# Moving part of an output product, half a matmul slot and a PSUM bank in a segment-recurrent attention kernel

## Chip, core and metric

The kernel runs on one core of a Trainium2 chip. The metric is device time in microseconds of one execution; the median of three runs of the kernel before is 957.34.

## What is computed

The reference has two blocks. Block A is attention over segments with a recurrent memory, block B a feed-forward network. Both have a residual connection around them and a layer norm (without gain) ahead of them. Cut to what matters here:

```python
# A: x (1,2048,640), 32 heads of 128, memory of M=8 rows, segments of 32 tokens -> 64 steps
mem = mem0
for s in range(64):
    h = concat([mem, x[:, 32*s:32*s+32]])            # 40 rows
    q, k, v = h@Wq, h@Wk, h@Wv                       # 32 heads x 128
    scores = q @ k.T * scale; masked: row i sees memory, and tokens up to itself
    o = softmax(scores) @ v @ Wo                     # 40 x 640
    mem = o[:, :8]                                   # goes into the next step
    outs.append(o[:, 8:])
# B: relu(x@w1 + b1)**2 @ w2 + b2
```

The next step's memory rows come out of this step's output product, so the 64 steps run one after the other.

## The kernel before

Only the memory rows and the first 24 tokens of a segment (`HD = 24`) are projected inside the step. The last 8 tokens of four segments (`TL = 8`) are projected together ahead of time as "tail units". Such units, and the output product of tail rows, stand in a list `fill`; `run(fill, n)` puts n of them into the instruction stream at fixed places of a step. A projection unit is one 128-row chunk of the contraction: four matmuls of 512 columns.

**Matmul shape.** Nearly all products of a step have 32 rows of output. They use a quarter of TensorE's columns: `proj` issues for each chunk c the four matmuls k = 0 to 3, each into 32 partitions of one PSUM tile, `ps[32*k:32*k+32, :]`. The scores do so for four groups g. In the profile these are the rows with `128*32`.

**One step** (`step(b, sp)`, s = 4b + sp) on PE, in the order in which the program issues it; all engines run their own queues in program order:

1. q0, k0, q1, k1: four projections (L234), 20 matmuls each. q1 goes into `potile(1)`, k0 into the one bank `ch`, the others into the pool `mm` of three banks.
2. scores(0) of the memory rows (L495), bank `ch`; the product v, first half, into `potile(0)`, 8 matmuls; token_scores(0) (L587); v first half, 12 more. ACT copies it out (L594).
3. v second half into an `mm` tile, first chunk: 4 matmuls; scores(1), bank `ch`, 16; second chunk, 4; token_scores(1), 16; last three chunks, 12. ACT copies it out (L608).
4. Some fill units; values(0) for the memory rows (L537 and L542; it needs pB0 from soft3); more fill units; values(1) (needs pB1 from soft2(1), L521).
5. The output product pw (`wo_rounds`, L270): 16 rounds of four plus four matmuls of 320 columns, in bank `ch`. Rounds 0 to 7 read the first half of the heads in `oT`, 8 to 15 the second half. ACT casts the first half of oT from values(0) (L246), DVE the second from values(1) (L244).
6. The rest of the fill units, then token_values of the step before (L421, L426).

On DVE and ACT the softmax of the memory rows runs beside this: soft1 is mx (DVE L501) and em (ACT L504), soft2 is rm, em, pm (DVE L510 to L518) and for n = 1 the transpose into pB1 (L521), soft3 is pT and four copies into pB0 (L526 to L529). After values(1), DVE has in its queue: causal mask (L612, issued before its cast of oT), cast of oT (L244), mxk, tk (L642, L644), zk, rk (L651, L653), and then `wo_out`: ACT copies two blocks of pw to otmp (L285, L286), DVE adds them (o, L287) and `mem_to_hT` transposes o into hT (L380), in two parts. The next step's q0 waits for hT.

All of this is an order written out by hand (`manual_schedule`). Step 0 (`ready`) and step 63 (`last`) differ; 62 steps in between have the form above.

Of the kernel before, what the change touches and what calls it, by code (L numbers as in the profile page):

```python
# [11 lines left out]
F32 = mybir.dt.float32  # L12
# [4 lines left out]
def kernel(  # L17
# [19 lines left out]
    M = A_mem0.shape[1]  # L37
# [12 lines left out]
    NK = SEG + M  # L50
# [13 lines left out]
    chn = ctx.enter_context(tc.tile_pool(name="chn", bufs=1, space=bass.MemoryType.PSUM))  # L64
# [11 lines left out]
    wv = wts.tile([128, DC * HE], BF16)  # L76
# [25 lines left out]
    oT = const.tile([128, H, NK], BF16)  # L102
# [5 lines left out]
    def head(p):  # L108

        n, g, j = p // 16, p // 4 % 4, p % 4  # L110
        return g * HG + j * 2 + n
# [59 lines left out]
    def rows_of(b, sp):  # L171
        at = HD + sp * SEG
        return lambda c: hTs[b % 2][:, c * CW + at:c * CW + at + SEG]
# [47 lines left out]
            nc.scalar.copy(out=rows_in(b).rearrange("p c (s t) -> p c s t", s=4)[:, :, :, 0:HD], in_=ptv[:, :, :, 0:HD])  # L221
        return out

    def proj(w, by, lhs, n, ps, c0, c1):

        if by == "columns":
            wr = w[:].rearrange("p (c g j n k e) -> p c n k g j e", c=DC, g=G, n=2, j=4, k=4)
        elif by == "half":
            wr = w[:].rearrange("p (c k j n e) -> p c n k j e", c=DC, k=G, n=2, j=4)
        else:  # L230
            wr = w[:].rearrange("p (c k n f) -> p c n k f", c=DC, k=G, n=2)
        for c in range(c0, c1):
            for k in range(4):
                nc.tensor.matmul(ps[32 * k:32 * k + 32, :], lhsT=lhs(c), rhs=wr[:, c, n, k], start=(c == 0), stop=(c == DC - 1))  # L234

    def mmtile():
        return mm.tile([128, 512], F32, tag="mm", name="ps")

    def potile(h):
        return pop.tile([128, 2, 512], F32, tag="po%d" % h, name="px%d" % h)[:, 0, :]  # L240
# [21 lines left out]
    def wo_rounds(lhs, pw, hs):  # L262

        for h in hs:
            for kh in range(2):
                for ch in range(2):
                    j = kh * 2 + ch
                    p = h // 8 * 16 + kh * 8 + h % 8
                    c0 = 32 * (1 - kh)
                    nc.tensor.matmul(pw[32 * j:32 * j + 32, c0:c0 + DH], lhsT=lhs(p), rhs=wov2[:, head(p), ch],  # L270
                                     start=(h == 0), stop=(h == 15))
# [22 lines left out]
    def run(q, n, held=None, stop=False):  # L294
        while n > 0 and q:
            out = q.pop(0)()
            if out and held is not None:
                held.append(out)
                if stop:
                    break  # L300
            elif out:
                out[1]()
            n -= 1
# [10 lines left out]
    def settle(held, tails):  # L314
        for out in [o for o in held if o[0] == tails]:
            held.remove(out)
            out[1]()
# [96 lines left out]
    def token_values(s, v, vt4, po):  # L414

        sp = s % 4
        pTk, pTx = back.pop()
        for i in range(HG):
            for g in range(G):
                r = slice(32 * g, 32 * g + 32)  # L420
                nc.tensor.matmul(po[0][g][:, i * 32:(i + 1) * 32], lhsT=v[r, i * E:(i + 1) * E], rhs=pTk[r, i, :],  # L421
                                 start=(i == 0), stop=False, skip_group_check=True)
        for u in range(2):
            for g in range(G):
                r = slice(32 * g, 32 * g + 32)
                nc.tensor.matmul(po[0][g][:, u * 128:(u + 1) * 128].rearrange("p (j q) -> p j q", q=32)[:, :, 0:TL],  # L426
                                 lhsT=vt4[r, sp, u, :], rhs=pTx[r, u], start=False, stop=True, skip_group_check=True)

    def token_out(s, po):
        for h in range(2):  # L430
            gs = slice(2 * h, 2 * h + 2)
            nc.scalar.copy(out=oTg[:, gs, :, :, 0:SEG],  # L432
                           in_=po[1][h][:, :, 0:256].rearrange("p g (n j q) -> p g n j q", n=2, q=32))
        nc.gpsimd.tensor_copy(out=oTts[s // 4 % 2][:, :, s % 4 * TL:(s % 4 + 1) * TL], in_=oT[:, :, 0:TL])
# [17 lines left out]
    def step(b, sp, v=None):  # L452
        s = b * 4 + sp
        last = s == NS - 1
        lhs = rows_of(b, sp)
        ready = v is not None
# [67 lines left out]
        def soft3(pm):  # L524
            pT = s1.tile([128, 2, 32], BF16, tag="pTt", name="pT")[:].rearrange("p u k -> p (u k)")
            nc.vector.transpose(out=pT, in_=pm)  # L526
            for g, copy in enumerate((nc.vector.tensor_copy, nc.scalar.copy, nc.gpsimd.tensor_copy, nc.gpsimd.tensor_copy)):
                r = slice(32 * g, 32 * g + 32)
                copy(out=pBs[0][r, g], in_=pT[r])  # L529
            return pBs[0]  # L530

        def values(n, pB, po):
            cols = po[:, 0, 0:128]
            for j in range(4):
                i = n * 4 + j
                for k in range(4):
                    nc.tensor.matmul(cols[32 * k:32 * k + 32].rearrange("p (g i m) -> p i g m", g=G, i=4)[:, j],  # L537
                                     lhsT=v[:, i * E + 32 * k:i * E + 32 * k + 32],
                                     rhs=pB[:, :, SEG + j * M:SEG + (j + 1) * M],
                                     start=(j == 0), stop=False, skip_group_check=True)  # L540
            for k in range(4):
                nc.tensor.matmul(cols[32 * k:32 * k + 32].rearrange("p (g a) -> p g a", g=G), lhsT=vt4[:, sp, n, 32 * k:32 * k + 32], rhs=pB[:, :, 0:SEG],  # L542
                                 start=False, stop=True, skip_group_check=True)
# [39 lines left out]
        def token_scores(n):  # L583
            skv = view()
            for j in range(4):
                for g in range(G):
                    nc.tensor.matmul(skv[32 * g:32 * g + 32, n * 4 + j, :], lhsT=qT[:, n * 16 + g * 4 + j, :],  # L587
                                     rhs=kT[:, n * 16 + g * 4 + j, :], start=True, stop=True,
                                     skip_group_check=True)

        token_scores(0)
        if not ready:
            proj(wv, "half", lhs, 0, ps0, 2, DC)
            nc.scalar.copy(out=v[:, 0:512], in_=ps0[:])  # L594
            ps1 = mmtile()
            proj(wv, "half", lhs, 1, ps1, 0, 1)
        if not last:
            pm0 = soft2(0)
            scores(1)
            soft1(1)  # L600
            pT0 = soft3(pm0)
        if not ready:
            proj(wv, "half", lhs, 1, ps1, 1, 2)
        token_scores(1)
        if not ready:
# [5 lines left out]
        def causal(skv):  # L611
            nc.vector.tensor_tensor(out=skv[:, :, M:NK], in0=skv[:, :, M:NK],  # L612
                                    in1=mask[:].unsqueeze(1).to_broadcast([128, HG, SEG]), op=ALU.add)
# [7 lines left out]
        if last:  # L621
            run(fill, max(1, (len(fill) - 3) // 2), held, True)
            token_values(s - 1, *prevs[-2], po)
            token_out(s - 1, po)
            settle(held, True)
            run(fill, 2, held)
            settle(held, True)
            causal(skv)
        else:
            ahead = 0 if ready else (len(fill) + 1) // 2  # L630
            left = len(fill) - ahead
            run(fill, ahead // 2, held, True)
            values(0, pT0, po[1][0])
            values_out(0, po[1][0])
            run(fill, len(fill) - left, held)
            values(1, pT1, po[1][1])
            causal(skv)
            values_out(1, po[1][1])
            settle(held, True)
# [19 lines left out]
                                op=ALU.mult)  # L659

        if not last:
            pw = chn.tile([128, 512], F32, tag="ch", name="pw")
            if ready:
                for k in range(4):
                    run(fill, SEG0[k])
                    wo_rounds(lambda p: oT[:, p, M:NK], pw, [2 * k + h for h in (0, 1, 8, 9)])
            else:
                wo_rounds(lambda p: oT[:, p, M:NK], pw, range(16))
            o = wo_out(pw, ((s + 1) // 4, (s + 1) % 4))
            if s > 1:  # L670
                store_main(o, s - 2)
            held = []
            run(fill, 100, held)
            if s:
                token_values(s - 1, *prevs[-2], po)
                token_out(s - 1, po)
            settle(held, True)
            for _, f in held:
                late.append((0.35, f, s + 1))
            tails_in((s + 1) // 4, (s + 1) % 4)  # L680
# [284 lines left out]
    for t in range(S // NT):  # L965
# [8 lines left out]
        for fc in range(FC):  # L974
            ps = mmtile()
# [8 lines left out]
            w = NT if fc < FFULL else HT  # L984
# [3 lines left out]
            if more and fc >= 1 and (fc - 1) // 3 < NK4:  # L988
                k, stage = divmod(fc - 1, 3)
# [30 lines left out]
        for q in range(NK4):  # L1020
# [6 lines left out]
            for hh in range(2):  # L1027
                k = pr + 2 * hh
# [44 lines left out]
```

## Time and profile before

| | us |
|---|---|
| median of 3 runs | 957.34 (956.87 to 958.79) |
| the profiled execution | 956.46 |
| its span in the profile | 954.60 |
| PE busy | 923.6 |
| DVE busy | 703.6 |
| ACT busy | 552.3 |
| POOL busy | 309.5 |

The span is the time from the first to the last instruction of the profiled execution; 1.86 us lie around it. "Busy" is the time in which at least one instruction of an engine runs. Matmuls overlap and their ends are modelled, so a busy PE can still be waiting for something; where that matters, the starts of matmuls in the timeline are compared with the time that the ones before them take. The granted TensorE clock was 0.998 of full speed over the run. The recurrent steps take most of the span, some 12 us each; the feed-forward network comes at the end.

### The profile page before, as it was taken

The numbers are of one execution on the slowest core, as the hardware profiler recorded it, in microseconds if no ns is written. First come the engines' busy times: TensorE is split into PE (matmuls) and PEld (weight loads), VectorE is DVE, ScalarE is ACT, GpSimd is POOL, SyncE is SP. The second block draws the span as 40 slices with busy tenths as digits, with TensorE's granted clock in tenths as the row PEclk, the third lists the DMA queues.
The fourth block names the chain that finished last, engine by engine and source line by source line (L and its number), as shares of the span: only waits on it lengthen the run. The fifth ranks groups of instructions, "written<-read, shape, count | busy, mean of one in ns | idle before, by whom it ended". The sixth has DMA issues, their size and how long they took to land.

```text
span 954.6 us, 55984 instructions
## 1 busy us (share of the span) xinstructions
PE 923.6 (97%) x24760; PEld 544.0 (57%) x24760; DVE 703.6 (74%) x2131; ACT 552.3 (58%) x1460; POOL 309.5 (32%) x1002
## 2 busy tenths in 40 slices
PE   5979999999999999999999999999999999999998
PEld 2445555655565656556565656565655555555555
DVE  5168888778877887877877787878787788556632
ACT  2546666666666666666666666666666666523321
POOL 2123333333333333333333333333333333353300
PEclk9999999999999999999999999999999999999999
DMA  9983201010101000100101010101010221633320
GB/s 352 402 265 70 38 18 27 16 30 13 23 20 28 16 21 24 21 25 11 34 17 23 14 31 14 32 12 33 8 32 8 54 43 21 203 108 88 94 56 28
DMA packets 65875, 56.66 MB, mean 59 GB/s; under 512 B 37384, under 2 KB 61712, under 8 KB 63712
## 3 DMA queue, kind: packets, MB, share of 16 engines
q1 hardware_dynamic: 65392, 52.74, 19.6%
q8 instruction: 194, 3.18, 1.4%
q14 instruction: 49, 0.40, 0.1%
q0 software_dynamic: 224, 0.33, 0.1%
q10 hardware_dynamic: 16, 0.01, 0.0%
HBM read 38.37 MB, written 9.44 MB: 50 GB/s over the span
## 4 chain that ended last, share of the span: by engine, by line
PE 80%; ACT 6%; DVE 5%; DMA 5%; SPq 2%; issue 1%; ACTq 0%
PE ps L234 23%; PE pw L270 15%; PE px L234 14%; PE pk L234 7%; PE y L1030 6%; PE ps L978 6%; ACT v L594 3%; PE ps L270 2%; DMA wq<-in_A_Wq_dram 2%; PE po L421 2%; ACT em L504 2%; SPq L151 2%; DVE pm L518 2%; PE po L537 2%; DVE pB L521 2%
## 5 line engine op out<-in xcount | busy, mean ns | idle before, releaser
L234 PEld LDWEIGHTS <-hT 128*32 128x32 bf16 x7680 | 178.9, 96 | 161.2 <-DVE hT L380 24.3
L270 PE MATMUL pw<-wo,oT 128*32 128x320 bf16 x4224 | 157.7, 299 | 2.5 <-DMA wo<-in_A_Wo_dram 1.0
L270 PEld LDWEIGHTS <-oT 128*32 128x32 bf16 x4224 | 120.0, 96 | 22.8 <-issue 3.7
L258 DVE STREAM_TRANSPOSE qT<-row 128x512 bf16<-128x512 bf16 x128 | 89.5, 699 | 44.1 <-ACT row L253 43.7
L234 PE MATMUL ps<-wv,hT 128*32 128x512 bf16 x1260 | 91.9, 377 | 0.0
L649 ACT ACTIVATE ek<-tk 128x320 bf16<-128x320 f32 x64 | 30.1, 470 | 101.9 <-DVE tk L644 101.9
L655 POOL TENSOR_TENSOR pkt<-ek,rk 128x64 bf16<-128x64 bf16 x64 | 18.8, 294 | 212.1 <-ACT otmp L286 176.0
L234 PE MATMUL px<-wv,hT 128*32 128x512 bf16 x1260 | 85.2, 377 | 0.0
L234 PE MATMUL ps<-wq,hT 128*32 128x512 bf16 x1260 | 81.3, 383 | 3.3 <-DVE hT L380 2.8
L234 PE MATMUL ps<-wk,hT 128*32 128x512 bf16 x1280 | 80.0, 379 | 0.0
L234 PE MATMUL px<-wq,hT 128*32 128x512 bf16 x1260 | 78.9, 379 | 0.0
L234 PEld LDWEIGHTS <-hTt 128*32 128x32 bf16 x1920 | 54.4, 97 | 42.2 <-issue 10.1
L234 PE MATMUL pk<-wk,hT 128*32 128x512 bf16 x1240 | 77.7, 379 | 0.0
L986 ACT ACTIVATE wv<-ps,b1f 128x512 bf16<-128x512 f32 (+1 forms) x56 | 37.6, 672 | 67.0 <-PE ps L978 66.5
L432 ACT CAST oT<-po 128x512 bf16<-128x512 f32 x128 | 68.7, 589 | 8.2 <-PE po L426 2.5
L441 POOL COPY qz<-qT 128x96 bf16<-128x96 bf16 x126 | 33.4, 265 | 111.4 <-DVE qT L258 111.4
L285 ACT COPY otmp<-pw 64x96 f32<-64x96 f32 (+2 forms) x129 | 28.8, 223 | 54.0 <-PE pw L270 33.4
L1030 PE MATMUL y<-wq,wk 128*128 128x320 bf16 x416 | 58.9, 299 | 0.2
L482 ACT CAST row<-ps 128x256 bf16<-128x256 f32 x126 | 40.7, 375 | 30.0 <-PE ps L234 29.1
L253 ACT ACTIVATE row<-ps 128x512 bf16<-128x512 f32 x93 | 54.8, 613 | 5.3 <-PE ps L234 4.0
L253 ACT ACTIVATE row<-px 128x512 bf16<-128x512 f32 x63 | 37.6, 597 | 32.2 <-PE px L234 32.2
L537 PEld LDWEIGHTS <-v 128*32 128x32 bf16 x2016 | 34.1, 94 | 34.7 <-issue 15.6
(138 smaller groups left out, 1886.1 us busy)
## 6 DMA issues: line engine op xcount, KB each, us to landing
wv<-in_A_Wv_dram SPq DMA_DIRECT2D x5, 1024.0 KB
wq<-in_A_Wq_dram SPq DMA_DIRECT2D x5, 1024.0 KB
wk<-in_A_Wk_dram SPq DMA_DIRECT2D x5, 1024.0 KB
wo<-in_A_Wo_dram SPq DMA_DIRECT2D x8, 640.0 KB
o_all<-o SPq DMA_DIRECT2D x256, 7.5 KB
vt<-vt_d SPq DMA_DIRECT2D x60, 64.0 KB
xt<-in_A_x_dram SPq DMA_DIRECT2D x19, 160.0 KB
wq<-in_B_w_dram SPq DMA_DIRECT2D x1, 2080.0 KB
```

Source lines behind the costliest of these rows:

```text
L234: nc.tensor.matmul(ps[32 * k:32 * k + 32, :], lhsT=lhs(c), rhs=wr[:, c, n, k], start=(c == 0), stop=(c == DC - 1))
L253: nc.scalar.mul(out=row, in_=ps, mul=scale)
L258: nc.vector.transpose(out=dst[:, n * 16:(n + 1) * 16, 0:32], in_=row.rearrange("p (h e) -> p h e", e=32))
L270: nc.tensor.matmul(pw[32 * j:32 * j + 32, c0:c0 + DH], lhsT=lhs(p), rhs=wov2[:, head(p), ch], start=(h == 0), stop=(h == 15))
L432: nc.scalar.copy(out=oTg[:, gs, :, :, 0:SEG], in_=po[1][h][:, :, 0:256].rearrange("p g (n j q) -> p g n j q", n=2, q=32))
L441: nc.gpsimd.tensor_copy(out=d.rearrange("p a (j f) -> p a j f", j=3)[:, :, :, 0:M], in_=src[:, :, 0:3, :])
L482: nc.scalar.copy(out=row[:, u * 256:(u + 1) * 256], in_=ps[:, u * 256:(u + 1) * 256])
L537: nc.tensor.matmul(cols[32 * k:32 * k + 32].rearrange("p (g i m) -> p i g m", g=G, i=4)[:, j], lhsT=v[:, i * E + 32 * k:i * E + 32 * k + 3 ...
L649: nc.scalar.activation(out=ek[:], in_=tk[:], func=ACT.Exp, scale=1.0)
L978: nc.tensor.matmul(ps[:], lhsT=w1[:, c, fc * 128:(fc + 1) * 128], rhs=hnT[:, c, :], start=(c == 0), stop=(c == DC - 1))
L986: nc.scalar.activation(out=r[:, 0:w], in_=ps[:, 0:w], func=ACT.Relu, bias=b1f[:, fc:fc + 1], scale=1.0)
L1030: nc.tensor.matmul(y[hh][:, 0:DH], lhsT=f1T[:, fc, k * 128:(k + 1) * 128], rhs=w2[:, fc, cs], start=(fc == 0 and not hf), stop=(fc == FFUL ...
```

## The change

Three edits, in the 62 steps of the ordinary form:

- The second half of v goes into `potile(1)`, the bank that q1 used earlier in the step, and takes no tile of the pool `mm`.
- Of the first chunk of that product, only matmuls k = 0 and 1 stand ahead of scores(1); k = 2 and 3 follow the scores, ahead of the second chunk. `proj` gets an argument `ks` for that.
- The tile pw is taken earlier, and rounds 0 and 1 of the output product (8 of 64 matmuls) are issued between the second group of fill units and values(1). The other 14 rounds stay where they were.

No instruction is added or taken away.

```diff
-    def proj(w, by, lhs, n, ps, c0, c1):
+    def proj(w, by, lhs, n, ps, c0, c1, ks=range(4)):
...
         for c in range(c0, c1):
-            for k in range(4):
+            for k in ks:
                 nc.tensor.matmul(ps[32 * k:32 * k + 32, :], lhsT=lhs(c), rhs=wr[:, c, n, k], start=(c == 0), stop=(c == DC - 1))
...
-            ps1 = mmtile()
-            proj(wv, "half", lhs, 1, ps1, 0, 1)
+            ps1 = potile(1)
+            proj(wv, "half", lhs, 1, ps1, 0, 1, range(2))
         if not last:
             pm0 = soft2(0)
             scores(1)
             soft1(1)
             pT0 = soft3(pm0)
         if not ready:
+            proj(wv, "half", lhs, 1, ps1, 0, 1, range(2, 4))
             proj(wv, "half", lhs, 1, ps1, 1, 2)
...
             run(fill, len(fill) - left, held)
+            pw = chn.tile([128, 512], F32, tag="ch", name="pw")
+            if not ready:
+                wo_rounds(lambda p: oT[:, p, M:NK], pw, range(2))
             values(1, pT1, po[1][1])
...
         if not last:
-            pw = chn.tile([128, 512], F32, tag="ch", name="pw")
...
-                wo_rounds(lambda p: oT[:, p, M:NK], pw, range(16))
+                wo_rounds(lambda p: oT[:, p, M:NK], pw, range(2, 16))
```

## The prediction

> **What bounds the kernel now.** I read the page first. PE is busy 97% of the span and holds 80% of the chain that ended last; the other engines have room.
>
> ```profile
> PE 923.6 (97%) x24760; PEld 544.0 (57%) x24760; DVE 703.6 (74%) x2131; ACT 552.3 (58%) x1460; POOL 309.5 (32%) x1002
> ...
> PE 80%; ACT 6%; DVE 5%; DMA 5%; SPq 2%; issue 1%; ACTq 0%
> ...
> L270 PE MATMUL pw<-wo,oT 128*32 128x320 bf16 x4224 | 157.7, 299 | 2.5 <-DMA wo<-in_A_Wo_dram 1.0
> L1030 PE MATMUL y<-wq,wk 128*128 128x320 bf16 x416 | 58.9, 299 | 0.2
> ```
>
> The last two lines decide this case. A matmul of 320 columns that fills a quarter of the array (128*32) lasts 299 ns, exactly as long as one that fills all of it (128*128). The first kind still costs only 157.7/4224 = 37 ns, the second 58.9/416 = 142 ns. So four quarter matmuls run side by side in one slot, and a quarter matmul by itself is no shorter than the slot. For 512 columns the timeline below gives the slot: 12 matmuls, three slots, from 418.99 to 419.63, so 0.215 us.
>
> PE's busy share hides its stops, since the ends are modelled. The waits name them:
>
> ```profile
> PEld L234 <- DVE hT L380: 24.3, 67, 1.5
> ...
> PE po L537 <- DVE pB L521: 3.4, 15, 0.5
> ...
> PE ps L234 <- ACT v L608: 2.4, 11, 0.2
> ```
>
> PE waits for the next step's rows (hT), for the second softmax of the memory rows (pB), and for the copy of v, which holds a buffer that a fill tile wants. The true sizes come from starts in the timeline. An ordinary step, first:
>
> ```profile
> 418.35 0.39 PE L234 MATMUL ps<-wv,hT 128*32 128x512 bf16 x4
> 418.57 0.27 PE L495 MATMUL sm<-kT,qz 128*32 128x40 bf16 x16
> 418.67 0.39 PE L234 MATMUL ps<-wv,hT 128*32 128x512 bf16 x4
> 418.88 0.27 PE L587 MATMUL ps<-kT,qT 128*32 128x40 bf16 x16
> 418.99 0.82 PE L234 MATMUL ps<-wv,hT 128*32 128x512 bf16 x12
> 419.63 0.60 PE L234 MATMUL ps<-wv,hTt 128*32 128x512 bf16 x8
> 420.06 0.27 PE L537 MATMUL po<-pB,v 128*32 128x32 bf16 x16
> 420.17 0.23 PE L542 MATMUL po<-pB,vt 128*32 128x128 bf16 x4
> 420.22 0.60 PE L234 MATMUL ps<-wv,hTt 128*32 128x512 bf16 x8
> 421.00 0.28 PE L537 MATMUL po<-pB,v 128*32 128x32 bf16 x16 [0.17 <-DVE pB L521]
> ...
> 421.15 2.36 PE L270 MATMUL pw<-wo,oT 128*32 128x320 bf16 x64
> 423.32 1.00 PE L270 MATMUL ps<-wo,oTt 128*32 128x320 bf16 x24
> ```
>
> The two fill slots from 420.22 are done at 420.65, yet the second memory values start at 421.00: 0.35 us idle, of which the view owns to 0.17. The same reading over the 62 steps that change gives 12.7 us in all before the second values. A step with the buffer wait:
>
> ```profile
> 407.98 0.28 PE L537 MATMUL po<-pB,v 128*32 128x32 bf16 x16
> 408.09 0.24 PE L542 MATMUL po<-pB,vt 128*32 128x128 bf16 x4
> 408.55 0.62 PE L234 MATMUL ps<-wk,hTt 128*32 128x512 bf16 x8 [0.23 <-ACT v L608]
> ```
>
> L542 issues its 128 columns in 0.05, so the fill could have gone at 408.14 and lost 0.41. Such waits sum to 6.5 us, in 18 steps, and are over 0.3 in 15 of them. Waits before the first values sum to 2.7.
>
> **Split of a slot (second scores "two matmuls sooner").** No matmul is added. But the slot at 418.35 now holds two of its four matmuls, and the scores follow. The scores' first matmul needs the quarter that the slot's first one occupies for 0.215, and matmuls start in program order in every row I looked at; so it starts at 418.57, as before, and two quarters stand idle. The other two matmuls then start at 418.67 with the first two of the next chunk; that chunk's last two take one slot more, from 418.88. All later PE work of the step is 0.215 us behind: 62 × 0.215 = 13.3 us, before what the waits swallow. By the Trainium skill (TensorE: Matmul & The Clock Gate, Part 3, "The mechanism") "MATMULs are pc-monotone in start AND end — strict FIFO, no reordering"; by that rule the price is the same 0.215, and the trace's order of starts agrees. Bounds for the price: nothing, if the scores can pass; two slots, 0.43, if the halves of the two chunks don't pair. I take one slot, by the two rows of the page. Even sooner scores would help little: em(1) on ACT starts at 419.22, and the copy of v's first half, ahead of it in ACT's queue, ends at 419.16 (418.57 plus 0.585).
>
> **Odd value product in the second query bank.** It leaves the three-buffer pool, so the fill tile no longer waits for the copy of v. Its new bank was read last by the copy of the odd q, over at 404.47 in the step where the product begins at 406.01: 1.5 us of cover, and its price, were that gone, would be the lateness itself. The second values share the bank, but need that copy of v anyway.
>
> **Two rounds ahead.** Eight of the 64 pw matmuls, 2 × 0.135 = 0.27 us (64 in 421.15 to 423.32), move before the second values. They use only the first half of oT, written by ACT's cast (L246), so PE has a new wait there; behind it are queued the second values, the rest of pw, and through them DVE's cast of oT, mxk, tk, zk, rk and then o, which makes hT. Their bank was last read by em(1), over at 419.60 in the step above and so 1.4 us before. No DMA and no POOL instruction moves.
>
> **An ordinary step, retimed.** The fill starts at 419.85, the first values at 420.28, the second fill ends at 420.86. The last v matmuls end at 419.81 + 0.215 = 420.02, and v's copy (ACT, 419.90 to 420.48 now) starts at 420.08. The cast of oT (420.45 to 420.72) follows the first values: 420.67 to 420.94. With 0.06 of hand-over (pB ends 420.95, values 421.00) the rounds start at 421.00, after 0.14 of waiting, and end at 421.27. The second values start at 421.27 instead of 421.00. pw has 56 left, 14 slots, 1.89 us, from 421.42: ended at 423.31, against 423.32. PE is level; the early rounds have paid for the slot. DVE is not: its cast of oT and all behind it shift by 0.27. rk ended at 423.92, and o started at 424.06, behind ACT's otmp. DVE starts an unrelated operation some 0.08 before the last one's end (causal 420.86, pB end 420.95), so there is 0.22 of slack: o and hT come 0.05 later, and hT released the next step at 424.69. Cost +0.05.
>
> **The step with the buffer wait.** Values(0) had waited from 407.72 to 407.98, which takes the slot in. The fill runs at 408.14 to 408.57. ACT's casts don't move (v 407.91, oT 408.39 to 408.66). Rounds 408.72 to 408.99; values(1) at 409.01, as now. pw ends 0.27 sooner, rk doesn't, and o moves from 412.08 to rk's end less 0.07, 411.86: −0.22.
>
> **Sum.** Of the 62 steps, 16 are like the first (wait before the second values over 0.3): 16 × 0.05 = 0.8. In 31 that wait is smaller and less is there to be swallowed; the same retiming gives +0.115 in the mean, 3.6. The 15 with the buffer wait give up to −0.22; I credit half, −0.11, as in each of them the slack of another engine must hold: −1.7. Sum +2.7 us, bounds +1.1 (full credit) and +4.4 (none). The profiled execution's 956.46 (its span 954.60 and 1.86 around it) becomes 959.2. It lay 0.88 under the median of the runs; on the median, 957.34 + 2.7 = **960.0 us**.
>
> **Rivals.** 0.2%, 1.9 us, is what can be told from no change.
> 1. *The split is free* (it ends faster). If the scores' matmuls on idle quarters could start at once and the halves filled in behind, no slot is lost. The ordinary step then has its cast at 420.45 to 420.72, rounds at 420.78, second values at 421.05, pw ended 0.22 sooner, and o held by rk at 423.90 instead of 424.06: −0.16. 47 × −0.16 − 15 × 0.22 = −10.8: 946.5. For it: the quarters do run side by side. Against: no row shows a later matmul starting ahead of an earlier one. From 0 to 0.215 the sum goes from −10.8 to +2.7, so it is not slower if the split costs under 0.17. In the Trainium skill (TensorEngine Tiling, "Key Properties") tiles "operate independently", which taken alone speaks for this; the trace can't show it, as every group in it is a whole four. 0.12.
> 2. *The waits swallow it.* If the cast of oT comes 0.05 sooner than retimed, as where ACT's casts overlap, DVE's slack holds in 16 steps (0), the 31 fall to +0.065 (2.0), and the buffer steps give −0.11 to −0.22 (−1.7 to −3.3): 956 to 957.6; with parts of it, 955 to 959.2. For it: 0.05 is near the hand-overs' size. Against: the cast waits for the first values, which are late. 0.36, of which 0.10 is faster by over 0.2%.
> 3. *Two slots.* If the split halves of two chunks don't pair, everything is another 0.215 late; DVE's slack is spent, so 47 steps pay +0.21 more and the 15 go to about −0.05: 4.4 + 9.9 − 0.8 = +13.5, 970.8. With one slot and no overlap on DVE behind rk, 47 × 0.08 more: 963.8. 0.12.
>
> **Chances.** Forecast case 0.40 (959.3 to 963), all of it slower; rivals 0.12, 0.36, 0.12. Faster 0.12 + 0.10 = 0.22; same 0.26; slower 0.40 + 0.12 = 0.52. Range 953 to 965: the free split (0.12) and the two slots' upper part (0.08) are left out.
>
> **What would show it.** Right: scores(1) still 0.215 behind the first v matmul of its chunk, token_scores' end 0.2 later; no wait on the copy of v before the second fill; a wait on ACT L246 before pw; the ordinary step, 11.98 now, at some 12.03 to 12.10; hT waits grown. Wrong: scores(1) 0.1 sooner (rival 1), or two extra slots before the last 12 v matmuls (rival 3).

## The result, and the profile after

The changed kernel takes 961.72 us (median of 22 runs, 958.91 to 964.76) beside 958.07 for the kernel before (22 runs, 955.95 to 962.55): a ratio of **1.0035, 95% interval [1.0024, 1.0046]**, slower by about 3.4 us. The forecast was 960.0, slower. The profiled execution took 960.2 us, its span 958.4.

The page of the changed kernel: the busy line, and the shares of the chain that ended last.

```profile
PE 928.9 (97%) x24760; PEld 564.6 (59%) x24760; DVE 703.8 (73%) x2131; ACT 553.9 (58%) x1460; POOL 311.0 (32%) x1002
...
PE 79%; DVE 10%; DMA 4%; ACT 2%; SPq 2%; issue 2%; DVEq 0%; POOL 0%; ACTq 0%
```

PE has nothing more to do, yet is busy 5.3 us longer, and DVE's share of the chain went from 5% to 10%. Its waits (engine, line, what it waited for: us in all, times, longest):

```profile
PEld L234 <- DVE hT L380: 33.1, 98, 1.5
...
DVE oT L244 <- PE po L542: 23.4, 60, 1.3
...
PEld L270 <- ACT oT L246: 21.3, 59, 0.6
```

The wait on the copy of v ahead of the fill is gone. The new wait on ACT's L246 ahead of pw is there, in 59 places. DVE now waits for the second memory values before its cast of oT (23.4 us in all, 4.1 before). PE's wait for hT grew from 24.3 to 33.1 us.

The chain of waits shows where the end of a step went. Before, from the step that the prediction retimed:

```profile
421.33 2.17 PE pw L270 x64
423.51 0.81 PE ps L270 x24
424.32 0.36 PE po L421 x32
```

PE itself was the chain. After, the same step:

```profile
421.81 0.39 PE pw L270 x8
422.20 0.09 PE po L537 x16
422.29 0.10 PE po L542 x4
422.40 0.02 issue
422.42 0.29 DVE oT L244
422.71 0.41 DVE mxk L646
...
423.14 0.50 DVE tk L648
...
424.23 0.50 DVE zk L655
...
424.75 0.06 DVE rk L657
424.81 0.05 issue
424.86 0.05 DVEq L287
424.91 0.04 issue
424.96 0.27 DVE o L287
```

The two early rounds (8 matmuls) push values(1) back, and from there DVE's softmax of the tokens, not pw, leads to o. In front of o stands a row of DVE's queue (DVEq), to which the experiments return.

The split slot, in the timeline of PE (start, duration, then the group; neighbours that interleave are cut into several rows):

```profile
418.53 1.02 PE L234 MATMUL px<-wv,hT 128*32 128x512 bf16 x11
419.33 0.28 PE L495 MATMUL sm<-kT,qz 128*32 128x40 bf16 x13
419.44 0.38 PE L234 MATMUL px<-wv,hT 128*32 128x512 bf16 x1
419.44 0.18 PE L495 MATMUL sm<-kT,qz 128*32 128x40 bf16 x1
419.45 0.38 PE L234 MATMUL px<-wv,hT 128*32 128x512 bf16 x1
419.45 0.19 PE L495 MATMUL sm<-kT,qz 128*32 128x40 bf16 x2
419.48 0.56 PE L234 MATMUL px<-wv,hT 128*32 128x512 bf16 x4
```

Two v matmuls (k = 2 and 3) start at 419.44 and 419.45 between scores that stand ahead of them in the program. In the starts of the single matmuls, k = 0 and 1 went at 419.161 and 419.168; the scores of groups 2 and 3 start at 419.333, and those of groups 0 and 1, which come first in the program, at 419.376, which is 419.161 + 0.215. So a quarter of the array starts its next matmul when that quarter is free, whatever the other quarters do. The scores of groups 2 and 3 did not wait for the slot. They waited for the second half of kT, of which DVE's transpose ended at 419.28:

```profile
418.51 0.77 DVE L485 STREAM_TRANSPOSE kT<-row 128x256 bf16<-128x256 bf16 x2
```

All that follows goes by this table of medians over some 60 steps, in us, each taken from the starts of the instructions in the trace (q0 is the first matmul of a step). Its last two rows are medians of the change of a step's length against the same step before: for the 15 steps whose fill had waited over 0.3 us for the copy of v ("buffer wait"), and for the other 47.

| | before | after | no split | split alone | bank alone | rounds alone |
|---|---|---|---|---|---|---|
| q0 to values(0) | 7.343 | 7.459 | 7.354 | 7.455 | 7.333 | 7.350 |
| q0 to pB1's end | 8.232 | 8.222 | 8.237 | 8.222 | 8.236 | 8.231 |
| pB1's end to values(1) | 0.054 | 0.287 | 0.112 | 0.053 | 0.146 | 0.201 |
| rk's end to o | 0.146 | 0.071 | 0.069 | 0.149 | 0.150 | 0.071 |
| otmp's end to o | 0.033 | 0.170 | 0.170 | 0.032 | 0.032 | 0.171 |
| values(1) to the next q0 | 3.698 | 3.624 | 3.622 | 3.699 | 3.697 | 3.625 |
| whole step | 11.986 | 12.133 | 11.995 | 12.042 | 12.080 | 12.064 |
| change, 15 steps with the buffer wait | | −0.145 | −0.233 | +0.123 | −0.090 | +0.107 |
| change, the other 47 | | +0.128 | −0.017 | −0.011 | +0.095 | −0.012 |

The profiled execution of "no split" was the longest of its 11 (956.48 us, median 953.46), and one early step alone took 2.9 us more in it than before; so its median of the whole step, 11.995, does not show the gain that its runs do.

### The profile page after: what moved, and what is told of

The parts are those of the page before. It is cut to its first block, busy times and chain, and to the rows that moved or that the text cites. A ratio compares the mean times of both kernels' runs of the same rounds, so it can differ in the third digit from the quotient of the medians.

```text
span 958.4 us, 55984 instructions
## 1 busy us (share of the span) xinstructions
PE 928.9 (97%) x24760; PEld 564.6 (59%) x24760; DVE 703.8 (73%) x2131; ACT 553.9 (58%) x1460; POOL 311.0 (32%) x1002
## 4 chain that ended last, share of the span: by engine, by line
PE 79%; DVE 10%; DMA 4%; ACT 2%; SPq 2%; issue 2%; DVEq 0%; POOL 0%; ACTq 0%
PE px L234 21%; PE ps L234 21%; PE pw L270 8%; PE pk L234 7%; PE y L1033 6%; PE ps L981 6%; PE ps L587 2%; PE ps L270 2%; DMA wq<-in_A_Wq_dram 2%; DVE zk L655 2%; DVE tk L648 2%; SPq L151 2%; ACT ek L653 2%; DVE mxk L646 2%; PE po L537 1%
## 5 line engine op out<-in xcount | busy, mean ns | idle before, releaser
L234 PEld LDWEIGHTS <-hT 128*32 128x32 bf16 x7680 | 188.0, 96 | 164.9 <-DVE hT L380 33.1
L234 PE MATMUL px<-wv,hT 128*32 128x512 bf16 x2520 | 177.2, 378 | 0.0
L270 PE MATMUL pw<-wo,oT 128*32 128x320 bf16 x4224 | 169.2, 299 | 3.9 <-ACT oT L246 1.0
L270 PEld LDWEIGHTS <-oT 128*32 128x32 bf16 x4224 | 110.7, 96 | 45.5 <-ACT oT L246 21.3
L234 PEld LDWEIGHTS <-hTt 128*32 128x32 bf16 x1920 | 61.8, 97 | 29.1 <-issue 3.5
L587 PEld LDWEIGHTS <-qT 128*32 128x32 bf16 x2048 | 44.4, 94 | 22.4 <-POOL qT L389 1.3
L495 PEld LDWEIGHTS <-qz 128*32 128x32 bf16 x2016 | 37.8, 95 | 24.2 <-issue 1.3
```

Of the source, the lines that this page charges most:

```text
L495: nc.tensor.matmul(sm[32 * g:32 * g + 32, 0:NK], lhsT=qz[:, p, :], rhs=kT[:, p, :], start=(j == 0), stop=(j == 3), skip_group_check=True)
```

## The experiments

Two theories were set against each other first. **S** is the prediction's: the split costs one slot of 0.215 us in each step, and o can start 0.08 before rk's end. **Q** came from the trace above: quarters run independently, so that the split costs about 0.1, and o doesn't start before rk has ended.

**No split.** The second bank and the early rounds alone:

```diff
-            proj(wv, "half", lhs, 1, ps1, 0, 1, range(2))
+            proj(wv, "half", lhs, 1, ps1, 0, 1)
...
-            proj(wv, "half", lhs, 1, ps1, 0, 1, range(2, 4))
```

> The changed kernel without the split: the first chunk of v's second half is whole again ahead of the second scores; the bank and the two early rounds stay. Theory S (the prediction's: the split costs one whole slot, 0.215 us in each of 62 steps, and DVE lets o start 0.08 before rk ends): the time falls by 13 us against the changed kernel, to some 947, ratio to before 0.989. Theory Q (the quarters of the array run on their own, so the split costs only some 0.1 us a step, and o can't start before rk has ended, so that the steps are held by DVE anyway): it falls by 4 to 6 us, to 955 to 957, ratio 0.997 to 0.999. In the trace, first v matmul of the second half to first memory value is 1.71 us again (1.82 with the split) under both; Q says that the wait of o for rk stays in most steps.

Measured: 953.46 us against 956.77, ratio 0.9965 [0.9953, 0.9976]. S is out, Q a little too timid. The other two edits gain 0.35%, and the split turns that into a loss: 1.0035 − 0.9965 = 0.007, 6.7 us, or 0.11 in each of 62 steps. The table says the same: values(0) 7.459 with it, 7.354 without.

**The split alone.** v's second half back in the pool (`ps1 = mmtile()`), all 16 rounds behind values(1).

> The kernel before with the split alone: two matmuls of the first chunk of v's second half go behind the second scores. Theory S (one slot of 0.215 us): the waits before the second memory values swallow it in some steps, not in those with the buffer wait; some +4.4 us, 962.5, ratio 1.0046. Theory Q (0.1 us a step): swallowed in nearly every step, +0 to +2 us, ratio 1.000 to 1.002. Scores no sooner by either.

Measured: 959.31, 1.0026 [1.0015, 1.0037], between the two and nearer to Q. Values(0) are 0.112 late, but pB1 ends where it did (8.222 beside 8.232) and values(1) wait for pB1, so much of the lateness is swallowed by that wait: the 47 steps without the buffer wait are as long as before (−0.011), and the cost lies in the other 15 (+0.123). Sooner scores gave nothing: pB1 ends 0.01 sooner.

**The bank alone.** `potile(1)`, the whole slot ahead of the scores, and all rounds behind values(1).

> The kernel before with the bank alone: v's second half goes into the second query bank. Both theories: the fill no longer waits for the copy of v in the 18 steps that had it, but the second memory values then wait for pB1 there; -1 to -3 us, ratio 0.997 to 0.999. If the buffer wait were worth its whole 6.5 us, ratio 0.993.

Measured: 961.61, 1.0048 [1.0035, 1.0062]. Both theories missed: an edit that only takes a wait away costs 4.6 us. The table has the place: values(1) start 0.146 after pB1's end, 0.054 before. The groups of line L537 (rows of PE's queue for weight loads: count, least, median and longest ns), kernel before:

```profile
L537 PEldq EVENT_SEMAPHORE  x63: 51/51/51, 54.3 to 807.3; - x63
```

and the bank alone, with its chain around values(1):

```profile
L537 PEldq EVENT_SEMAPHORE  x125: 51/51/51, 53.0 to 812.2; - x125
```

```profile
459.86 0.46 DVE pB L521
460.32 0.14 issue
460.45 0.28 PE po L537 x16
```

62 more such rows, one a step (the 63 before stand ahead of values(0)). With v's second half in the bank into which values(1) write, these wait for three engines: DVE (pB1), ACT (the copy of v) and PE (the product that used the bank). The third wait stands as a row of its own ahead of the weight load. The first load and the first matmul of values(1), before and with the bank alone:

```profile
457.04 0.09 PEld L537 LDWEIGHTS <-v 128*32 128x32 bf16 x1 [0.21 <-ACT v L608]
...
457.50 0.28 PE L537 MATMUL po<-pB,v 128*32 128x32 bf16 x16 [0.17 <-DVE pB L521]
```

```profile
460.42 0.20 PEld L537 LDWEIGHTS <-v 128*32 128x32 bf16 x16 [0.73 <-ACT oT L246]
460.45 0.28 PE L537 MATMUL po<-pB,v 128*32 128x32 bf16 x16 [0.26 <-DVE pB L521]
```

Before, the first weight load had waited for ACT alone and was over when pB1 came (457.04 to 457.13, pB1's end 457.45), and the matmul followed 0.05 later. Now the row waits for pB1 (460.35 to 460.40), then the load starts (460.42), then the matmul (460.45).

**The rounds alone.** v's second half in the pool, its first chunk whole, and rounds 0 and 1 ahead of values(1).

> The kernel before with the two early rounds alone: 8 pw matmuls go ahead of the second memory values. Theory S (o may start 0.08 before rk ends): the ordinary step gains some 0.05 to 0.16, -3 to -8 us, ratio 0.992 to 0.997. Theory Q (o not before rk has ended): the second values come later by up to 0.05, DVE's chain to o with them, and nothing is gained; -2 to +1 us, ratio 0.998 to 1.001, with o released by rk in most steps instead of by ACT's otmp.

Measured: 958.59, 1.0018 [1.0006, 1.0030], just above what Q said. In the median values(1) come 0.147 later (8.433 after q0 beside 8.286), and the rest of the step gives back only 0.073, because o then waits for rk. The wait of the fill for the copy of v is still there (2.5 us in 11 places, beside 2.4 before). The median mixes two kinds of steps. In the 47 without the buffer wait the rounds alone do what rounds and bank do together (−0.012 beside −0.017). The loss lies in the other 15 (+0.107 beside −0.233): there the fill still starts late, the early rounds stand behind it, and values(1) behind both come 0.26 later than before, where with the new bank they come 0.13 sooner.

So bank and rounds are each a loss alone and a gain together, and each mends the other's loss. The bank takes the late fill from the rounds. The rounds take the third wait from the bank: they already wait for ACT's cast of oT, which comes after the copy of v in ACT's queue, so values(1) are left with two waits, and the extra row is gone (63 again without the split).

**Is it the third wait?** The bank alone, with one tiny matmul that takes the wait for ACT:

```diff
             pw = chn.tile([128, 512], F32, tag="ch", name="pw")
+            if not ready:
+                nc.tensor.matmul(pw[0:32, 32:40], lhsT=v[:, 512:544], rhs=v[:, 512:520], start=True, stop=True,
+                                 skip_group_check=True)
             values(1, pT1, po[1][1])
```

> The bank change alone (1.0048 of before), with one more matmul of 8 columns ahead of the second memory values that reads v's second half and writes a place of pw that is overwritten later; it adds nothing to the result. It takes the wait for ACT's copy of v off the second values, which are then left with two waits (DVE, PE). Theory W (with three engines to wait for, the program put an EVENT_SEMAPHORE row ahead of values(1)'s weight load, and load and matmul came 0.146 us after pB1's end instead of 0.054): values(1) starts 0.05 to 0.07 after pB1's end, about 0.09 x 60 = 5 us less than the bank alone: 0.997 to 1.000. Rival B (it is the bank, written again right after it was read, whatever the waits): 0.13 to 0.15 after pB1's end, 1.004 to 1.007.

Measured: 955.42 against 957.34, 0.9980 [0.9969, 0.9991]. Values(1) start 0.056 after pB1's end in the median, there are 63 rows again, and one matmul more in each step made the kernel 0.7% faster than without it. It is the wait, not the bank. And it is the wait's own row, not that the weight load comes late: here too the load waits for pB1, and load and matmul then start together, 0.054 and 0.056 after pB1's end in the median (0.115 and 0.146 with the bank alone).

```profile
423.00 0.17 PEld L537 LDWEIGHTS <-v 128*32 128x32 bf16 x16 [0.37 <-DVE pB L521]
```

```profile
423.00 0.28 PE L537 MATMUL po<-pB,v 128*32 128x32 bf16 x16 [0.17 <-DVE pB L521]
```

**Does rk hold o?** Without the split, rk and its two readers on POOL moved between the two halves of `wo_out`:

```diff
-    def wo_out(pw, then=None):
+    def wo_out(pw, then=None, between=None):
...
                 mem_to_hT(o, *then, cs)
+            if between and c0 == 0:
+                between()
...
-        rk = s1.tile([128, HG], F32, tag="rk", name="rk")
-        nc.vector.reciprocal(out=rk[:], in_=zk[:])
...
+        def rk_part():
+            rk = s1.tile([128, HG], F32, tag="rk", name="rk")
+            nc.vector.reciprocal(out=rk[:], in_=zk[:])
...
-            o = wo_out(pw, ((s + 1) // 4, (s + 1) % 4))
+            o = wo_out(pw, ((s + 1) // 4, (s + 1) % 4), rk_part)
```

> The changed kernel without the split of the slot (0.9965 of before), and with DVE's reciprocal rk and its two POOL readers issued between the two halves of wo_out instead of ahead of it. Theory Q (o starts only 0.07 us after rk's end, and with the two early rounds it is rk that holds o while otmp has been ready for 0.17 us): o comes 0.13 us sooner in each of some 60 steps, 0.133 x 60 = 8 us less: 0.987 to 0.991 of before. Theory S (the prediction's: o could overlap the end of rk and has slack behind it, so rk's place in the queue is worth nothing): 0.9955 to 0.9975, as without the move.

Measured: 947.60 against 957.41, **0.9900 [0.9881, 0.9920]**: the fastest kernel of this case, faster than both. o starts 0.032 after otmp, values(1) to the next q0 is 3.427 (3.622 without the move). DVE's order at the end of a step in its timeline, and the shares of the chain:

```profile
407.13 0.26 DVE L287 TENSOR_TENSOR o<-pw,otmp 128x96 bf16<-128x96 f32 x1
407.43 0.28 DVE L382 STREAM_TRANSPOSE hT<-o 128x96 bf16<-128x96 bf16 x1
407.63 0.16 DVE L659 RECIPROCAL rk<-zk 128x8 f32<-128x8 f32 x1
407.88 0.23 DVE L287 TENSOR_TENSOR o<-pw,otmp 128x64 bf16<-128x64 f32 x1
```

```profile
PE 90%; DMA 4%; DVE 2%; SPq 2%; ACT 1%; issue 1%; POOL 0%; DVEq 0%; ACTq 0%; POOLq 0%
```

rk fills a gap of DVE between the halves, and the chain is PE's again: DVE 2%, 10% after.

**The same move in the kernel before.**

> The kernel before, with the same move of rk, pkt and pk alone. Theory Q: there o is ended by otmp (0.033 us after its end, 0.146 after rk's), so rk's place is worth little: 0.998 to 1.001. Rival R (rk's place costs DVE or POOL the same whatever the rounds do): 0.987 to 0.993.

Measured: 958.99 against 957.41, 1.0011 [0.9997, 1.0026]. There o waited for otmp, and the place of rk is worth nothing. It is the early rounds that make rk the bound.

**One early round.** No split, `range(1)` and `range(1, 16)`.

> The changed kernel without the split, and with one round of the output product ahead of the second memory values instead of two. Theory W (the one round is enough to take the wait for ACT off the second values, so no third wait stands ahead of them; values(1) then starts 0.05 to 0.06 us after pB1's end as before, and 0.05 sooner than with two rounds): 0.994 to 0.9965 of before. Rival (each early round is worth its 0.135 us of slot on the path through pw): 0.998 to 1.002.

Measured: 951.48, 0.9935 [0.9917, 0.9953]: one round does better than two (0.9965 [0.9953, 0.9976], in another set of runs; the intervals just touch), and by a little more than W said. Values(1) are back at 0.055 after pB1's end and 8.292 after q0, and values(1) to q0 is 3.627, hardly longer than with two rounds (3.622), whose second one went into the slack behind rk.

**One early round, and rk moved.**

> No split, one early round (0.9935 of before alone) and rk between the halves of wo_out (0.990 with two early rounds). Theory P (with rk out of the way the end of the step is pw's last matmul and otmp, so it is PE's work that counts: one round fewer ahead puts 0.135 us back behind values(1), which start 0.06 sooner): 0 to 0.075 us a step slower than with two rounds: 0.990 to 0.995. Rival A (the two gains are of different places and add): 0.9935 - 0.0065, so 0.985 to 0.988.

Measured: 950.91 against 957.34, 0.9939 [0.9926, 0.9952]: P. With rk gone from the chain, the round that is not ahead costs its time behind values(1) (3.566 beside 3.427, 0.139; a round is 0.135), and the two gains don't add.

**The whole change, and rk moved.**

> The whole change (1.0035 of before) with rk between the halves of wo_out. Theory Q: o is again ended by otmp instead of rk, 0.13 us sooner a step, as in the kernel without the split, and the split's own cost stays 0.10 to 0.12 a step: 0.9965 to 0.999. Rival (the split's lateness had been hidden in part behind rk, so the gain is smaller or the split dearer, up to 0.215 a step): 1.000 to 1.003.

Measured: 953.16, 0.9960 [0.9946, 0.9973], Q's side, and a little past it. Against the same kernel without the split (0.9900) the split costs 0.6%, 5.7 us or 0.09 in each step.

**The split the other way round.** k = 2 and 3 ahead of the scores, `range(2, 4)`, and k = 0 and 1 behind them, `range(2)`.

> The changed kernel with k = 2 and 3 of the chunk ahead of the second scores, and k = 0 and 1 behind them: the scores' first group in the program now meets an idle quarter. Theory Q (quarters run independently): the groups 0 and 1 start 0.1 to 0.2 us sooner than in the changed kernel against the first v matmul of that chunk (0 to 0.1 behind it instead of 0.215), and the whole is 0.999 to 1.004 of before, as em(1) waits for ACT's copy of v anyway. Theory S (matmuls start in program order and a split costs a whole slot): the scores start 0.215 behind that matmul, and the time is the changed kernel's, 1.003 to 1.005.

Measured: 962.04 against 957.41, 1.0045 [1.0028, 1.0061], a time that lies in S's range. The starts are what Q said. PE's timeline:

```profile
421.26 0.19 PE L495 MATMUL sm<-kT,qz 128*32 128x40 bf16 x2
421.27 0.38 PE L234 MATMUL px<-wv,hT 128*32 128x512 bf16 x2
421.44 0.25 PE L495 MATMUL sm<-kT,qz 128*32 128x40 bf16 x10
```

The first two scores start beside, even 0.01 ahead of, the two v matmuls that stand before them in the program (median −0.008; 0.173 in the changed kernel, 0.215 before). Then they stop until 421.44, because the scores of groups 2 and 3 wait for DVE's second half of kT (its two transposes run from 420.61 to 421.38), and what is behind a waiting matmul in the program doesn't start, though its quarter is free. Both quarters lose that time.

**The split, filled.** k = 2 and 3, then the scores of groups 0 and 1, then k = 0 and 1, then groups 2 and 3:

```diff
-            proj(wv, "half", lhs, 1, ps1, 0, 1, range(2))
+            proj(wv, "half", lhs, 1, ps1, 0, 1, range(2, 4))
...
-            scores(1)
+            scores(1, None if ready else lambda: proj(wv, "half", lhs, 1, ps1, 0, 1, range(2)))
...
-            proj(wv, "half", lhs, 1, ps1, 0, 1, range(2, 4))
```

Here `scores` issues groups 0 and 1, then its second argument, then groups 2 and 3.

> The changed kernel with the split filled: matmuls k = 2 and 3 of v's chunk first, then the scores of groups 0 and 1 (whose half of kT comes first), then matmuls k = 0 and 1, then the scores of groups 2 and 3, so that each quarter of the array has work at each point. Theory Q (each quarter starts what is next for it as soon as it is free; the split costs because two quarters stand idle until DVE's second kT half): the first scores start within 0.05 us of the first v matmul of the chunk, the last at 0.28 to 0.32, values(0) start 7.34 to 7.38 after q0 as without a split (7.354; 7.459 in the changed kernel), and the time is that of the kernel without the split: 0.995 to 0.998 of before. Rival H (a slot given up in two halves costs 0.1 us or more whatever stands between them): values(0) at 7.44 to 7.48, 1.002 to 1.005.

Measured: 955.32 against 957.63, 0.9976 [0.9962, 0.9989]. Values(0) start 7.354 after q0, to the thousandth as without a split, and the interval overlaps that of the kernel without a split (0.9965 [0.9953, 0.9976]). In the median the first score stands 0.007 ahead of the first v matmul and the last one 0.297 behind it. A slot in two halves costs nothing that can be told here, if each quarter has something to do.

## Why the prediction was right

In direction and size it was right: 960.0, measured 961.72 (+2.7 us forecast; +3.65 between the medians). Its parts were not all right. Two errors of some 7 us each cancelled: the split cost 6.7 us instead of the 13.5 between rival 1's −10.8 and the forecast's +2.7, and without it the kernel took 953.5 instead of rival 1's 946.5. That the sum came so close is luck.

- **The split as a whole slot.** The term that was mis-sized: 0.215, 62 × 0.215 = 13.3 us. Measured 0.11 a step, 6.7 us. The prediction took the order of starts from rows in which every group was a whole four, which can't show the difference, as its rival 1 itself said. The rule from the Trainium skill that it quoted (TensorE: Matmul & The Clock Gate, Part 3, "The mechanism": starts and ends in strict program order) does not hold here for the starts: scores at 419.333 start ahead of scores at 419.376, and v matmuls at 419.435 and 419.451 ahead of scores at 419.455 and 419.463, though the program has the later starters first. The other page of the Trainium skill that it named (TensorEngine Tiling, "Key Properties": tiles operate independently) agrees with the trace, with the limit that a matmul which waits for another engine holds those behind it. What the split costs is two quarters that stand idle from 419.16 to 419.33 for kT.
- **The slack of DVE at the end of the step**, 0.22, the second mis-sized term. o was to overlap rk's end by 0.08; in the median it starts 0.07 after it, so 0.075 was there (0.146 before, 0.071 after), and of the 0.27 that the rounds move only 0.074 came back. The prediction had this as one clause in its rival 3 (one slot, and no overlap behind rk). The trace points to the reason, by the rows of DVE's queue (EVENT_SEMAPHORE, L287) between rk and o: of the steps in which rk bounds o, those with one such row start 0.08 before rk's end (7), those with two at 0.00 (18), those with three 0.07 after it (28). The slack of 0.22 was there where one row stands: the way from values(1) to the next q0 is 0.27 shorter than before in the median of those steps, 0.14 with two rows and 0.07 with three. No run takes rows away, so this is read from the steps and not tested. The rows are waits of o for older stores and for PE. Before, they lay hidden behind the wait for otmp. The Trainium skill (Perfetto Trace Analysis, "Identifying Dependency Chains") says that an instruction waiting on several engines may get such instructions ahead of it; the trace agrees, 50 ns each in the median here.
- **The bank.** "Its price, were that gone, would be the lateness itself" was right about the cover of the old reader, and the wait that it removed is gone. That the new bank adds a third wait to values(1) was not seen. In the whole change the early rounds hide it; alone it is 0.09 a step. The sum was spared by luck.
- **The step with the buffer wait.** It was credited with −0.11 in 15 steps, at most −0.22. Those 15 steps are 0.14 shorter than before in the mean, and 0.18 without the split; the other 47 are 0.13 longer (0.09 by the forecast's 4.4 us). This term held.
- **Rivals.** A free split was to give 946.5. Without any split the kernel takes 953.5. Rival 1 let o start 0.07 before rk's end, and mostly it doesn't; so a split at no cost (also shown with the filled split) is not enough for its time. With rk out of the way it is 947.6, near rival 1's sum, but that is another kernel, in which rk no longer stands ahead of o. Rival 3's two slots did not occur. Rival 2's swallowing is seen with the split alone, where values(1) wait for pB1; in the whole change values(1) come 0.23 later than before in the 47 ordinary steps.
- **"What would show it".** The step that was retimed came to 12.07, inside the 12.03 to 12.10 that was named, and the median step to 12.133, just over it; the last token_scores start 0.18 later and the waits for hT grew, as said. "Scores(1) still 0.215 behind" was wrong for half of the groups (0.173), which is where the slot's size could have been read.

## What to carry to other kernels

Before a wait is counted as removed, count the waits of the instruction that inherits the buffer: one engine more to wait for may cost more than the wait that went, and an earlier instruction that has to wait for that engine anyway can take it over. When work is moved ahead of a step on the critical path, look at what else ends there: here the second early round paid only after a 0.2 us reciprocal had been taken out of the queue in front of o (0.9900 with two rounds and 0.9939 with one, beside 0.9965 and 0.9935). And where matmuls fill a quarter of the array, count time for each quarter by itself, and give every quarter work that is ready.

## What was not expected of the hardware

- Quarter matmuls start out of program order across quarters: scores 0.008 us ahead of v matmuls that stand before them in the program. Up to the point at which one waits for another engine: then the later ones wait too (0.18 us in the reversed split).
- A third engine to wait for costs 0.09 us ahead of a group of matmuls (0.146 beside 0.054): a row of 51 ns in the queue, behind which the weight load and then the matmul start later. That the load is no longer done ahead of time costs nothing by itself (0.056 with the tiny matmul).
- On DVE, with each further wait row ahead of o its start lies 0.07 to 0.09 us later against rk's end (−0.083, 0.003, 0.072 in the median).
